# Transposing the last two tiles of batch 2 by DMA instead of TensorE, and holding the loads of batch 4 until they have landed

## The chip, the cores and the metric

The kernel runs on one core of one Trainium2 chip. The metric is device time in microseconds (us) of one execution. Before the change it is 290.95 us, the median of 3 runs (290.88 to 290.97). A profiled execution also has a *span*: from its first to its last instruction in the trace. The span is about 1.8 us shorter than the time.

## The reference

Per batch (8 of them) and head (8), linear attention without a softmax, an RMS norm, then one MLP block over the joined heads:

```python
kv = einsum('bhsd,bhse->bhde', k, v)            # 64 x 64 per head, s = 576
out = einsum('bhsd,bhde->bhse', q, kv)
x = out / sqrt(mean(out**2, -1) + 1e-6) * g_norm     # then heads joined: 576 x 512 per batch
xn = (x - mean(x)) / sqrt(var(x) + 1e-6) * g_ln
y = x + relu(xn @ w_ch1) @ w_ch2                 # 512 -> 2048 -> 512
```

## The kernel before

TensorE (PE) runs the two dense products batch after batch: `mm1` (`xT` by `w1`, L412) and `mm2` (`m` by `w2`, L428). The attention of later batches is cut into small pieces, which an agenda drops between groups of dense matmuls. A *slot* is one such group; a batch has 32. DVE (VectorE) and ACT (ScalarE) do the elementwise work, POOL (GpSimd) and SP (SyncE) issue most transfers, and PEld is PE's weight load. PE's products lie in PSUM until an *eviction* copies them out. A transfer tells of its landing by a *completion semaphore*, a counter that others wait for. Every tile of 128 rows of x must be turned (transposed) before `mm1` can use it, by PE through PSUM and an ACT copy, or by a DMA transpose on the SP queue:

```python
def turn(self, on_pe):
    dst = self.blk[2][:, :, self.ts * 128:(self.ts + 1) * 128]
    if on_pe:
        tp = ps_m.tile([128, nK, 128], bf16, tag="misc", name="tp")
        for kk in range(nK):
            nc.tensor.transpose(tp[:, kk, :], self.xc_t[:, kk * 128:(kk + 1) * 128], identity)
        nc.scalar.copy(dst, tp)
    else:
        nc.sync.dma_start_transpose(dst, self.xc_t)
...
def turn_q_dma(b):                       # q of a batch: a DVE copy, then one large DMA transpose
    q_p = ...
    nc.vector.tensor_copy(q_p.rearrange("p j h d -> p h j d"), q_in[b % NB])
    ...
    nc.sync.dma_start_transpose(q_t..., q_p...)
...
def load_batch(b, after=None):           # six loads on the POOL queue
    if after is not None:
        nc.gpsimd.tensor_copy(gate, after)   # one element: POOL waits for whoever writes `after`
    load(k_in[b % NB], k, b); load(v_in[b % NB], v, b); load(q_in[b % NB], q, b)
...
def plan_tile(s, make, turn_at, on_pe):  # attention of one tile from slot s on, turned at slot turn_at
    ...
at(36, lambda: kv_of(2))
at(36.5, lambda: turn_q_dma(2))
for j, s, tn in ((0, 44, 50), (1, 48, 54), (2, 53, 61), (3, 58, 67)):
    plan_tile(s, lambda j=j: main_tile(2, j), tn, j > 1)      # tiles 2 and 3 on PE
plan_tile(62, lambda: rem_tile(1), 69, False)
...
for b in range(3, B):
    s = 32 * b
    at(47 if b == 3 else s - 60,
       lambda b=b: load_batch(b, qts[b - 1][:1, J, HP - 1, 127:]))
    d = -41 if b == 3 else -45
    at(s + d, lambda b=b: kv_of(b))               # needs all of k and v of batch b
    at(s + d + 1.7, lambda b=b: turn_q_dma(b))
    for j in range(J):
        o = s + d + (10 if b == 3 else 13) + 5 * j
        plan_tile(o, lambda b=b, j=j: main_tile(b, j), o + 6, False)
```

Each 128-row output tile is evicted by DVE (L433) and stored by two transfers (L446, L447), nearly all on the SP queue; the last three pairs are shared by SP and ACT.

Of the kernel before, what the change touches and what calls it, by code (L numbers as in the profile page):

```python
# [14 lines left out]
def kernel(  # L15
# [11 lines left out]
    nc = tc.nc  # L27
# [10 lines left out]
    nK = Dm // 128  # L38
    nDe = Dh // 128
    HP = H // 2  # L40
# [3 lines left out]
    J, JJ, JP = 4, 5, 9  # L44
# [47 lines left out]
    def load(dst, t, b, h0=0, h1=H):  # L92
        nc.gpsimd.dma_start(dst[:64, h0:h1], lo(t, b, h0, h1))
        nc.gpsimd.dma_start(dst[64:, h0:h1, :J], up(t, b, h0, h1))

    def load_batch(b, after=None):
        if after is not None:
            nc.gpsimd.tensor_copy(gate, after)  # L98
        load(k_in[b % NB], k, b)
        load(v_in[b % NB], v, b)  # L100
        load(q_in[b % NB], q, b)
# [20 lines left out]
    gate = consts.tile([1, 1], bf16)  # L122
# [34 lines left out]
    load_w2(0)  # L157
    load_w2(1)
    load_batch(1)
    load_w2(2)  # L160
    load_w2(3)


    qts, held, blks, rstds, m1s, q_ps = {}, {}, {}, {}, {}, {}
# [35 lines left out]
    def turn_q_dma(b):  # L200
        q_p = kv_in.tile([128, JJ, H, D], bf16, tag="qp", bufs=2)
        nc.vector.tensor_copy(q_p.rearrange("p j h d -> p h j d"), q_in[b % NB])
        q_t = qt_pool.tile([128, JJ, HP, 128], bf16, tag="qt", name="qt")
        nc.sync.dma_start_transpose(
            q_t.rearrange("p j hp t -> p (j hp) t"), q_p.rearrange("p j h d -> p (j h d)"))
        qts[b] = q_t
# [31 lines left out]
    def kv_of(b):  # L238
        kv_ps = ps_m.tile([128, HP, D], f32, tag="misc", name="kv_ps")
        kvp = held[b] = kv_pack[b % 4]  # L240
        for hp in range(HP):
            for j in range(JJ):
                for hh in range(2):
                    h = 2 * hp + hh
                    nc.tensor.matmul(kv_ps[hh * D:hh * D + D, hp, :],  # L245
                                     lhsT=k_in[b % NB][:, h, j, :], rhs=v_in[b % NB][:, h, j, :],
                                     start=(j == 0), stop=(j == JJ - 1))
        nc.scalar.copy(kvp[:D, :, :D], kv_ps[:D])  # L248
        nc.scalar.copy(kvp[D:, :, D:], kv_ps[D:])

    def new_block(n, bufs):
        x_blk = xpool.tile([128, 4, Dm], f32, tag=f"x{n}", bufs=bufs, name="x_blk")
        st_blk = xpool.tile([128, 3, 4], f32, tag=f"st{n}", bufs=bufs, name="st_blk")
        xT_blk = xpool.tile([128, nK, 512], bf16, tag=f"xT{n}", bufs=bufs, name="xT_blk")
        return x_blk, st_blk, xT_blk
# [98 lines left out]
    def main_tile(b, j, pool=None, tag="ops"):  # L354
        q_t, kvp = qts[b], held[b]
        if b not in blks:
            blks[b] = new_block("main", 3)
        return Tile([(slice(0, 128), lambda hp: q_t[:, j, hp, :], kvp)], blks[b], j, pool, tag)

    def rem_tile(b):  # L360
        mms = []
        for half, bb in enumerate((b - 1, b)):
            qt, kp = qts.pop(bb), held.pop(bb)
            mms.append((slice(half * 64, (half + 1) * 64),
                        lambda hp, qt=qt: qt[:, J, hp, :64], kp))
        if "rem" not in blks:
            blks["rem"] = new_block("rem", 1)
        return Tile(mms, blks["rem"], b // 2)

    def plan_tile(s, make, turn_at, on_pe):  # L370
        box = []

        def first():
            t = make()
            box.append(t)
            t.o()
            t.sq()
            t.red()

        def second():  # L380
            t = box[0]
            t.y()
            t.x()
            t.xc()

        def third():
            box[0].var()

        def fourth():
            box[0].turn(on_pe)  # L390

        at(s, first)
        at(s + 2, second)
        at(s + 6, third)
        at(turn_at, fourth)
# [22 lines left out]
    def rstd_of(b):  # L418
        rstd = work.tile([128, 4], f32, tag="rstd", bufs=3, name="rstd")
        nc.scalar.activation(rstd, blks[b][1][:, 2, :], func=AF.Sqrt, scale=1.0 / Dm, bias=eps_sb)  # L420
        nc.vector.reciprocal(rstd, rstd)  # L421
        rstds[b] = rstd
# [45 lines left out]
    def at(slot, fn):  # L468
        agenda.setdefault(int(slot), []).append((slot, fn))
# [119 lines left out]
    def next_loads():  # L589
        nc.gpsimd.memset(k_in[0][64:, :, J], 0.0)  # L590
        nc.gpsimd.memset(v_in[0][64:, :, J], 0.0)
        load_batch(2)
# [30 lines left out]

    at(36, lambda: kv_of(2))
    at(36.5, lambda: turn_q_dma(2))
    for j, s, tn in ((0, 44, 50), (1, 48, 54), (2, 53, 61), (3, 58, 67)):
        plan_tile(s, lambda j=j: main_tile(2, j), tn, j > 1)
    plan_tile(62, lambda: rem_tile(1), 69, False)
    at(78, lambda: rstd_of(2))

    for b in range(3, B):
        s = 32 * b
        at(47 if b == 3 else s - 60,
           lambda b=b: load_batch(b, qts[b - 1][:1, J, HP - 1, 127:]))
        d = -41 if b == 3 else -45
        at(s + d, lambda b=b: kv_of(b))
        at(s + d + 1.7, lambda b=b: turn_q_dma(b))
# [3 lines that stand above are left out]
        if b % 2:  # L641
            plan_tile(s - 14, lambda b=b: rem_tile(b), s - 8, False)
        at(s + 14, lambda b=b: rstd_of(b))
# [59 lines left out]
```

## Time and profile before

| what | value |
|---|---|
| time, median | 290.95 us |
| span of the profiled run | 289.16 us |
| PE busy | 97% of the span |
| chain of waits that ended last | 91% PE |
| first product of the kernel (kv of batch 0) starts | 8.27 us |
| last eviction ends | 286.10 us |

The page of the kernel before: its first lines (busy us, share of the span, instructions) and the shares of the chain that ended last.

```profile
span 289.2 us, 5765 instructions
PE 279.8 (97%) x2289; PEld 158.9 (55%) x2315; DVE 149.8 (52%) x331; ACT 155.4 (54%) x338; POOL 40.9 (14%) x68
...
PE 91%; DMA 2%; DVE 2%; ACT 2%; issue 1%; DVEq 0%; POOLq 0%
```

PE is the limit. Only what leaves its stream, or makes it stand still, moves the time. The next fence is PE's timeline of the kernel before around the two tiles (start us, duration us, what).

```profile
78.95 0.39 PE L347 MATMUL tp<-identity,xc 128*128 128x128 bf16 x4
79.17 1.03 PE L428 MATMUL p<-w_sb,m 128*128 128x512 bf16 x4
...
82.22 1.04 PE L412 MATMUL p<-xT_blk,w_sb 128*128 128x256 bf16 x8
83.31 0.40 PE L270 MATMUL o_ps<-kv_pack,qt 128*128 128x128 bf16 x4
...
85.29 0.39 PE L347 MATMUL tp<-identity,xc 128*128 128x128 bf16 x4
85.51 0.71 PE L412 MATMUL p<-xT_blk,w_sb 128*128 128x256 bf16 x5
```

Four transposes last 0.39 us from the first start to the last end, but the next matmul starts 0.22 us after the first of them: that is what they cost. Note too the 1.09 us between the starts at 82.22 and 83.31. Eight matmuls of 256 columns at about 0.109 us need only 0.87. That gap of 0.22 us turned out to matter. The list of waits of the kernel before has it (us in total, times, longest) not at PE but at PEld, the weight load, which I had passed over:

```profile
PEld L270 <- DMA qt<-q_p: 0.3, 1, 0.3
```

POOL's timeline of the kernel before shows the hold of batch 4's loads: one copy that waits for the q transpose of batch 3, then the first load.

```profile
83.38 0.18 POOL L98 COPY gate<-qt 1x1 bf16<-1x1 bf16 x1 [16.93 <-DMA qt<-q_p]
84.57 0.68 POOL L93 DMA_DIRECT2D k_in<-in_k_dram  x1 [1.01 <-PE o_ps L270]
```

The landing times in the trace put the last v load of batch 4 at 97.60 us; PE starts `kv_of(4)` at 100.67.

### The profile page before, as it was taken

The numbers are of one execution on the slowest core, as the hardware profiler recorded it, in microseconds if no ns is written. First come the engines' busy times: TensorE is split into PE (matmuls) and PEld (weight loads), VectorE is DVE, ScalarE is ACT, GpSimd is POOL, SyncE is SP. The second block draws the span as 40 slices with busy tenths as digits, with TensorE's granted clock in tenths as the row PEclk, the third lists the DMA queues.
The fourth block names the chain that finished last, engine by engine and source line by source line (L and its number), as shares of the span: only waits on it lengthen the run. The fifth ranks groups of instructions, "written<-read, shape, count | busy, mean of one in ns | idle before, by whom it ended". The sixth has DMA issues, their size and how long they took to land.

```text
span 289.2 us, 5765 instructions
## 1 busy us (share of the span) xinstructions
PE 279.8 (97%) x2289; PEld 158.9 (55%) x2315; DVE 149.8 (52%) x331; ACT 155.4 (54%) x338; POOL 40.9 (14%) x68
## 2 busy tenths in 40 slices
PE   7889999999999999999999999999999999999995
PEld 3579755995569644445444444444444444444444
DVE  5774028838987783765366925762578300220022
ACT  3477854985469832882288418920894076016500
POOL 8522520031032003200410022000000000000000
PEclk9999999999999999999999999999999999999999
DMA  7999999569999929996997179937202510131033
GB/s 215 199 208 202 201 203 206 125 103 196 151 168 129 178 53 165 184 164 123 144 211 102 39 146 204 170 79 161 54 18 54 111 36 0 39 82 27 0 74 73
DMA packets 64890, 36.10 MB, mean 125 GB/s; under 512 B 32860, under 2 KB 59868, under 8 KB 64864
## 3 DMA queue, kind: packets, MB, share of 16 engines
q0 software_dynamic: 28528, 17.76, 46.0%
q1 hardware_dynamic: 35824, 17.25, 31.3%
q10 hardware_dynamic: 512, 0.72, 0.7%
q8 instruction: 18, 0.29, 0.4%
q14 instruction: 8, 0.07, 0.1%
HBM read 36.71 MB, written 9.44 MB: 160 GB/s over the span
## 4 chain that ended last, share of the span: by engine, by line
PE 91%; DMA 2%; DVE 2%; ACT 2%; issue 1%; DVEq 0%; POOLq 0%
PE p L428 43%; PE p L412 42%; PE o_ps L270 3%; DMA v_in<-in_v_dram 2%; PE kv_ps L245 2%; ACT m L415 1%; DVE x_blk L288 0%; DVE xc L546 0%; PE tp L347 0%; ACT sq L276 0%; ACT xT_blk L349 0%; PE tp L170 0%; ACT rms L307 0%; DVE ss L512 0%; PE tp L553 0%
## 5 line engine op out<-in xcount | busy, mean ns | idle before, releaser
L412 PE MATMUL p<-xT_blk,w_sb 128*128 128x128 bf16 (+2 forms) x1017 | 131.4, 285 | 0.8
L428 PE MATMUL p<-w_sb,m 128*128 128x512 bf16 (+2 forms) x590 | 126.8, 368 | 1.6 <-issue 1.0
L415 ACT ACTIVATE m<-p 128x512 bf16<-128x512 f32 x144 | 85.4, 596 | 43.9 <-PE p L412 41.8
L412 PEld LDWEIGHTS <-w_sb 128*128 128x128 bf16 x1024 | 78.6, 98 | 44.5 <-issue 1.1
L428 PEld LDWEIGHTS <-m 128*128 128x128 bf16 x608 | 56.8, 98 | 61.7
L433 DVE SCALAR_TENSOR_TENSOR o_sb<-p,rstd,x_blk 128x512 f32<-128x512 f32 (+2 forms) x38 | 27.3, 721 | 53.2 <-PE p L428 47.6
L276 ACT ACTIVATE sq<-o_ps 128x512 f32<-128x512 f32 x35 | 20.9, 596 | 42.1 <-PE o_ps L270 42.1
L297 DVE TENSOR_REDUCE ss<-sq 128x8 f32<-128x512 f32 x35 | 23.7, 678 | 11.4 <-ACT sq L276 11.4
L339 ACT ACTIVATE dev<-x_blk,st_blk 128x512 f32<-128x512 f32 x36 | 25.7, 714 | 4.6 <-DVE st_blk L325 4.4
L331 DVE SCALAR_TENSOR_TENSOR xc<-x_blk,st_blk,g_ln_sb 128x512 bf16<-128x512 f32 x34 | 25.6, 752 | 1.2
L302 DVE TENSOR_TENSOR y<-o_ps,inv 128x512 f32<-128x512 f32 x33 | 22.8, 692 | 3.0
L321 DVE SCALAR_TENSOR_TENSOR x_blk<-y,g_norm_sb 128x512 f32<-128x512 f32 x33 | 22.8, 692 | 1.1
L314 DVE RECIPROCAL inv<-rms 128x8 f32<-128x8 f32 x36 | 7.2, 201 | 24.8 <-ACT rms L307 24.8
L421 DVE RECIPROCAL rstd<-rstd 128x4 f32<-128x4 f32 x9 | 1.6, 174 | 34.7 <-ACT rstd L420 34.7
L98 POOL COPY gate<-qt 1x1 bf16<-1x1 bf16 x5 | 0.9, 176 | 113.2 <-DMA qt<-q_p 113.2
L307 ACT ACTIVATE rms<-ss,eps_sb 128x8 f32<-128x8 f32 x36 | 10.7, 297 | 8.0 <-DVE ss L297 7.7
L270 PEld LDWEIGHTS <-qt 128*128 128x128 bf16 (+1 forms) x156 | 10.2, 100 | 7.3 <-issue 1.7
L270 PE MATMUL o_ps<-kv_pack,qt 128*128 128x128 bf16 (+1 forms) x156 | 13.7, 220 | 0.1
L197 PE MATMUL p<-fill_sb 128*128 128x512 bf16 x26 | 7.8, 449 | 1.3 <-DVE eps_sb L137 1.2
L339 ACT ACTIVATION_READ_ACCUMULATOR dev<-x_blk,st_blk 128x1 f32 x36 | 6.9, 190 | 0.0
L248 ACT CAST kv_pack<-kv_ps 64x256 bf16<-64x256 f32 x7 | 2.6, 365 | 7.2 <-PE kv_ps L245 7.2
L245 PEld LDWEIGHTS <-k_in 128*64 128x64 bf16 x280 | 5.0, 112 | 2.6 <-issue 2.5
(79 smaller groups left out, 116.5 us busy)
## 6 DMA issues: line engine op xcount, KB each, us to landing
out_dram<-o_sb SPq DMA_DIRECT2D x70, 128.0 KB, 2.4
w_sb<-in_moe_w_ch_dram POOLq DMA_DIRECT2D x8, 512.0 KB, 14.0
k_in<-in_k_dram POOLq DMA_DIRECT2D x7, 320.0 KB, 5.8
v_in<-in_v_dram POOLq DMA_DIRECT2D x7, 320.0 KB, 10.2
q_in<-in_q_dram POOLq DMA_DIRECT2D x7, 320.0 KB, 13.0
q_in<-in_q_dram POOLq DMA_DIRECT2D x8, 256.0 KB, 13.3
k_in<-in_k_dram POOLq DMA_DIRECT2D x7, 256.0 KB, 7.4
v_in<-in_v_dram POOLq DMA_DIRECT2D x7, 256.0 KB, 11.0
```

The costliest lines, as they stand in the source:

```text
L245: nc.tensor.matmul(kv_ps[hh * D:hh * D + D, hp, :], lhsT=k_in[b % NB][:, h, j, :], rhs=v_in[b % NB][:, h, j, :], start=(j == 0), stop=(j = ...
L270: nc.tensor.matmul(flat[rows, hp * 128:(hp + 1) * 128], lhsT=lhsT_of(hp), rhs=kvp[:, hp, :], start=True, stop=True)
L276: nc.scalar.activation(self.sq_t, self.o_ps, func=AF.Square)
L297: nc.vector.tensor_reduce(self.ss, self.sq_t, axis=AX.X, op=ALU.add)
L302: nc.vector.tensor_mul(self.y_t, self.o_ps, self.inv().to_broadcast([128, H, D]))
L321: nc.vector.scalar_tensor_tensor(x_blk[:, ts].rearrange("p (h d) -> p h d", h=H), in0=self.y_t, scalar=1.0, in1=g_norm_sb.to_broadcast([12 ...
L331: nc.vector.scalar_tensor_tensor(self.xc_t, in0=x_blk[:, self.ts], scalar=st[:, 1, self.ts:self.ts + 1], in1=g_ln_sb, op0=ALU.add, op1=ALU ...
L339: nc.scalar.activation(dev, x_blk[:, ts], func=AF.Square, bias=st[:, 1, ts:ts + 1], accum_out=st[:, 2, ts:ts + 1])
L412: nc.tensor.matmul(p1[:, i, :], lhsT=w1_sb[:, kk, de * 128:(de + 1) * 128], rhs=blk[2][:, kk, sl], start=(kk == 0), stop=(kk == nK - 1))
L415: nc.scalar.activation(m1[:, de0:de0 + per, sl], p1, func=AF.Relu)
L428: nc.tensor.matmul(p2[:, c0:c1], lhsT=m1s[b][:, de, ts * 128:(ts + 1) * 128], rhs=w2_sb[:, de, c0:c1], start=(de == 0), stop=(de == nDe - 1))
L433: nc.vector.scalar_tensor_tensor(o_sb[:, c0:c1], in0=p2[:, c0:c1], scalar=rstds[b][:, ts:ts + 1], in1=blks[b][0][:, ts, c0:c1], op0=ALU.mu ...
```

## The change

The intent is to take the remaining PE transposes of batch 2 out of PE's stream. A DMA transpose is slow beside loads (in the kernel before one landed 9.7 us after its issue beside the loads of batch 4, the quickest 2.4 us), so the loads of batch 4 are held until tile 3's has landed. Tile 3 also moves to slightly earlier slots.

```diff
-    def load_batch(b, after=None):
-        if after is not None:
-            nc.gpsimd.tensor_copy(gate, after)
+    def load_batch(b, *after):
+        for element in after:
+            nc.gpsimd.tensor_copy(gate, element)
...
-    for j, s, tn in ((0, 44, 50), (1, 48, 54), (2, 53, 61), (3, 58, 67)):
-        plan_tile(s, lambda j=j: main_tile(2, j), tn, j > 1)
+    for j, s, tn in ((0, 44, 50), (1, 48, 54), (2, 53, 61), (3, 57.5, 64)):
+        plan_tile(s, lambda j=j: main_tile(2, j), tn, False)
...
-           lambda b=b: load_batch(b, qts[b - 1][:1, J, HP - 1, 127:]))
+           lambda b=b: load_batch(b, qts[b - 1][:1, J, HP - 1, 127:],
+                                  *([blks[2][2][:1, nK - 1, 511:]] if b == 4 else [])))
```

## The prediction

> **What bounds the kernel now.** TensorE. The page has PE busy 279.8 of 289.2 us (97%) at full granted clock; the chain of waits that ended last is 91% PE, mostly the two dense products (L428 43%, L412 42%). The list of waits has about 4 us of PE waits, most in the start-up. DVE (52%), ACT (54%) and the DMA engines are not the limit. Time falls only by what leaves PE's stream, and grows only by a transfer that makes PE stand still.
>
> **What the change removes.** Tiles 2 and 3 of batch 2 are no longer transposed on PE: 8 transposes and 8 weight loads, and two ACT evictions of 0.58 us. In the timeline the four transposes of a tile take 0.39 us from first start to last end, but they are pipelined: at 78.95 and at 85.29 us the surrounding product is displaced by 0.22 us each. All on PE's path: 0.44 us. PE did not wait for the evictions: worth nothing.
>
> **What it adds.** Two DMA transposes on the SP queue (issue 1.2 us, landing 2.4 us after issue at best, 3.8 median, 10.4 beside loads) and one tiny POOL copy. The order on SP is fixed: tile 2's goes between two pairs of output stores, tile 3's behind the second pair, before the one of the remainder tile. From before's issue times (q transpose until 81.4, stores 81.5 to 82.7) I work out: tile 2 issued at about 82.7, tile 3 at about 85.2, landed at 85.3 and 87.8. PE needs them at slot 72, about 90.1 us: slack of some 2 us, no wait, as no load is beside them. The Trainium skill, "DMA: Bandwidth & Descriptors", section "SWDGE vs HWDGE vs iDMA", says that these two feed different queues inside each DMA engine and take turns there; the trace agrees (a transpose beside loads landed after 9.7 us, one alone after 2.4).
>
> **What it moves.** The six loads of batch 4 begin at about 88.4 instead of 84.57 us. Before, the last v load landed 13.0 us after the first issue, at 97.60, and PE began kv of batch 4 at 100.67: slack 3.1 us, and the loads lose 3.8. But two transposes and a stretch of almost no traffic (91 to 93 us) lay in those 13 us; batches 3 and 6 took 9.3 and 10.0 us. After, the remainder tile's transpose is out of the way; I expect 10 to 12 us, so landing at 98.5 to 100.5, PE being there at 100.2. Most likely no wait, with one chance in three of a PE wait of about 1 us at kv of batch 4, never made up. q lands by 105 us, before its copy at about 106.
>
> **Sum.** 290.95 - 0.44 + about 0.1 of expected stall = 290.6 us. Range 290.1 to 291.6. Faster by 2% (5.8 us): 0.01; within 2%: 0.98; slower: 0.01.
>
> **What would show it.** PE instructions 16 fewer; no transposes at 79 and 85 us; POOL's hold ends near 88 us; first product of columns 256 to 511 of batch 2 without a wait; v of batch 4 landed before kv starts (right), or a PE wait for DMA v_in (wrong by its length).
>
> **What would make it wrong.** Tile 3's transpose landing later than 90 us (then PE waits at slot 72 and the loads slip further); loads of batch 4 taking 13 us again; the late q of batch 4 holding DVE, and through it the stores and the transpose of q; tile 3, a slot earlier, making DVE late with an eviction.

## The result, and the profile after

The changed kernel took 291.41 us, median of 4 runs (291.22 to 291.64), beside 290.94 us for the kernel before. The ratio is 1.0017, with a 95% interval from 0.9999 to 1.0034. (A ratio is the mean time of one kernel's fast runs over that of the other's of the same rounds, so it is not quite the ratio of the medians.) It is the same within 2%, and inside the predicted range, but the expected gain of 0.35 us is a loss of 0.47.

I cut each profiled execution into four pieces, and this cut decides nearly everything below:

- *head*: from the start of the span to the first kv product (code that the change does not touch);
- *body*: from there to the end of the last eviction;
- *end*: from there to the end of the span;
- *outside*: time less span.

The first two lines are of the kernel before, from the timelines of PE and DVE: the first kv product and the last eviction.

```profile
8.27 0.19 PE L224 MATMUL even<-v_in,k_in 64*64 64x64 bf16 x1 [1.50 <-DMA v_in<-in_v_dram]
...
285.75 0.35 DVE L433 SCALAR_TENSOR_TENSOR o_sb<-p,rstd,x_blk 128x128 f32<-128x128 f32 x1 [0.54 <-PE p L428]
```

The same two, and the span line of the page, of the changed kernel:

```profile
span 289.6 us, 5755 instructions
...
8.63 0.19 PE L224 MATMUL even<-v_in,k_in 64*64 64x64 bf16 x1 [0.52 <-DMA v_in<-in_v_dram]
...
285.86 0.35 DVE L433 SCALAR_TENSOR_TENSOR o_sb<-p,rstd,x_blk 128x128 f32<-128x128 f32 x1 [0.54 <-PE p L428]
```

| piece, us | before | changed | difference |
|---|---|---|---|
| head | 8.27 | 8.63 | +0.36 |
| body (285.75 + 0.35 - 8.27, and so on) | 277.83 | 277.58 | -0.25 |
| end (spans 289.16 and 289.64 unrounded) | 3.07 | 3.43 | +0.36 |
| outside (profiled run: 290.94 and 291.64 less span) | 1.78 | 2.00 | +0.22 |

The heads differ, so a time read in one profile compares with one in another only after the heads are taken off.

So the change gains in the body, as it was meant to, though less than the 0.44 us of PE work removed. It loses in two places that the prediction never looked at: the end, and outside the span. PE's timeline of the changed kernel shows where the gain shrank:

```profile
80.63 1.90 PE L428 MATMUL p<-w_sb,m 128*128 128x512 bf16 x8
82.36 1.04 PE L412 MATMUL p<-xT_blk,w_sb 128*128 128x256 bf16 x8
83.65 0.40 PE L270 MATMUL o_ps<-kv_pack,qt 128*128 128x128 bf16 x4 [0.24 <-DMA qt<-q_p]
83.88 2.35 PE L412 MATMUL p<-xT_blk,w_sb 128*128 128x256 bf16 x20
```

Both groups of transposes are gone. But from 82.36 to 83.65 it is 1.29 us, where before it was 1.09. Counted from the first kv product, PE starts these eight matmuls at 73.73 us, before at 73.95: arriving 0.22 us earlier, it waits 0.2 us longer for the q transpose of batch 3. That transpose is issued by a chain (an eviction, two stores, the q copy on DVE) that runs before the saved work and so does not become earlier: from the first kv product it is issued at 69.96 us, before at 69.95.

POOL's timeline of the changed kernel shows the new hold. The loads begin at 90.06 us:

```profile
88.88 0.18 POOL L98 COPY gate<-xT_blk 1x1 bf16<-1x1 bf16 x1 [4.98 <-DMA xT_blk<-xc]
90.06 0.68 POOL L93 DMA_DIRECT2D k_in<-in_k_dram  x1 [1.01 <-PE p L412]
```

The last v load landed at 99.71 us, PE started `kv_of(4)` at 100.78, and no wait appears there. The two DMA transposes landed 2.5 us after their issue. (PE's counts on the page fall from 2315 weight loads to 2307, as predicted, and from 2289 matmuls to 2282; a trace can miss a few matmuls.)

For the end, the list of waits of the SP queue, first of the kernel before:

```profile
SPq L698 <- DMA out_dram<-o_sb: 1.2, 2, 0.8
```

and of the changed kernel (us in total, times, longest):

```profile
SPq L699 <- DMA out_dram<-o_sb: 1.5, 1, 1.5
```

After its last store SP waits for the completion semaphores of all queues. In the trace's records these are nine instructions, each reading two semaphores in a fixed order, about 0.06 us apart. The transfers of SP and ACT take turns on eight of these semaphores. In the kernel before the last two stores complete on the two read last: SP has passed all the others while it waited, stops twice (for the landing of the second-last and of the last pair), and is done 0.14 us after the last landing. In the changed kernel two more SP transfers have turned the rotation by two. The last two stores now complete on semaphores read second and third, SP stops at the second for 1.5 us, and still has to read the other seven after the last landing; it is done 0.51 us after it.

### The profile page after: what moved, and what is told of

Read it like the earlier page. It is cut to its first block, busy times and chain, and to the rows that moved or that the text cites. A ratio compares the mean times of both kernels' runs of the same rounds, so it can differ in the third digit from the quotient of the medians.

```text
span 289.6 us, 5755 instructions
## 1 busy us (share of the span) xinstructions
PE 280.8 (97%) x2282; PEld 158.7 (55%) x2307; DVE 149.8 (52%) x331; ACT 154.4 (53%) x336; POOL 41.4 (14%) x69
## 4 chain that ended last, share of the span: by engine, by line
PE 69%; DMA 17%; issue 9%; POOL 2%; DVE 1%; POOLq 0%; DVEq 0%
PE p L428 33%; PE p L412 33%; DMA q_in<-in_q_dram 8%; DMA w_sb<-in_moe_w_ch_dram 5%; DMA v_in<-in_v_dram 3%; PE o_ps L270 2%; DMA qt<-q_p 2%; PE kv_ps L245 1%; POOL q_in L94 0%; DVE o_sb L433 0%; DVE q_p L202 0%; POOL v_in L93 0%; POOL v_in L94 0%; POOL k_in L93 0%; POOL q_in L93 0%
## 5 line engine op out<-in xcount | busy, mean ns | idle before, releaser
L197 PE MATMUL p<-fill_sb 128*128 128x512 bf16 x26 | 9.1, 512 | 1.3 <-DVE eps_sb L137 1.2
```

## The experiments

All ran correct. The table has every run: head, body and end in its profiled execution, *outside* as the mean of its runs (for the kernel before its profiled run; its later runs give means of 1.77 to 1.80), medians of the time, and the median of the kernel before in the same rounds.

| run | head | body | end | outside | time | before, same rounds |
|---|---|---|---|---|---|---|
| before | 8.27 | 277.83 | 3.07 | 1.78 | 290.94 | |
| changed | 8.63 | 277.58 | 3.43 | 2.02 | 291.41 | 290.94 |
| e1_before_plus2 | 9.05 | 277.79 | 3.43 | 1.75 | 291.35 | 291.23 |
| e2_after_plus6 | 8.32 | 277.58 | 3.04 | 1.96 | 290.97 | 291.23 |
| e3_after_nohold | 8.20 | 285.36 | 3.42 | 1.99 | 298.99 | 291.23 |
| e4_after_oldslots | 8.20 | 277.63 | 3.41 | 1.76 | 291.06 | 291.23 |
| e5_after_early_q | 8.26 | 277.19 | 3.40 | 2.02 | 290.82 | 291.12 |
| e6_after_best | 8.20 | 279.12 | 3.07 | 1.98 | 292.48 | 291.12 |
| e7_tile2_alone | 8.20 | 277.82 | 3.15 | 1.81 | 291.03 | 291.12 |
| e8_combined | 8.27 | 277.16 | 3.04 | 2.00 | 290.46 | 290.84 |
| e9_before_early_q | 8.95 | 277.60 | 3.06 | 1.78 | 291.38 | 290.84 |
| e10_combined_oldslots | 8.35 | 277.15 | 3.06 | 1.76 | 290.33 | 290.84 |
| e11_after_again | 8.18 | 277.57 | 3.44 | 1.98 | 291.19 | 290.90 |
| e12_before_2memsets | 8.18 | 277.61 | 3.05 | 2.02 | 290.85 | 291.01 |

Each kernel has one profiled execution, the changed kernel two. Where kernels differ only in what should not touch the body, it agrees to about 0.04 us (277.83 and 277.79 for before and e1; 277.58, 277.58 and 277.57 for changed, e2 and e11), and the end to about 0.04. The head does not: 8.18 to 9.05, and single times of the kernel before run from 290.77 to 291.91. So the pieces, not the medians, tell these experiments apart.

### Two and six more small transfers: the end (e1, e2)

Undo the suspected cause without the change, and cause it without the change.

```diff
+    spare = consts.tile([8, D], f32)
...
+    for i in range(2):          # e1, in the kernel before; range(6) in e2, in the changed kernel
+        nc.sync.dma_start(spare[i:i + 1, :], g_norm.rearrange("(a d) -> a d", a=1))
```

> The kernel before with two tiny extra transfers on the SP queue at the start, and nothing else. Theory A (end): the changed kernel loses at its end because two more transfers of the SP and ACT queues turn the rotation of completion semaphores by two, so that the last stores complete on the semaphores that SP reads second of nine, and SP still has to read the other seven, one after the other, after the last landing. Then this kernel loses the same at its end: time from the last eviction's end to the end of the span 3.4 us instead of 3.06, total about 291.3. Theory B (middle): the changed kernel's loss comes from its middle or is chance; then this kernel stays at 290.95, with 3.06 us at the end.

> The changed kernel with six tiny extra transfers on the SP queue at the start, so that with its own two the rotation is turned by eight, which is none. Theory A: the end takes 3.06 us again instead of 3.43, total 0.36 us under the changed kernel, about 291.05, or 290.7 if the 0.37 us that its profiled run lost at the start (v landing later) was chance. Theory B: no difference to the changed kernel, 291.4.

In e1 the end is 3.43 us and the body unchanged (277.79): two transfers that do nothing, 280 us earlier, cost the same 0.36 us. In e2 the rotation is turned by eight in all, which is none, and the end is 3.04 us. Theory A holds, theory B falls. The list of SP waits of e1:

```profile
SPq L701 <- DMA out_dram<-o_sb: 1.5, 1, 1.5
```

and of e2:

```profile
SPq L702 <- DMA out_dram<-o_sb: 1.2, 2, 0.8
```

The median of e1 (ratio 1.0003, interval 0.999 to 1.0017) would not have shown this; on that chip the head was scattering.

### Without the hold (e3)

```diff
-                                  *([blks[2][2][:1, nK - 1, 511:]] if b == 4 else [])))
+                                  *[]))
```

> The changed kernel without the hold: loads of batch 4 start when the q transpose of batch 3 has landed, as before. If the hold is what makes the DMA transposes cheap: loads start near 84.6 us, tile 3's transpose is issued near 86 and lands beside them after some 9.7 us, near 96; PE needs it near 90.3 and stands still for about 5 us: total 295 to 297. Rival (the hold is idle, a transpose ahead of most load traffic lands in time): no PE wait, total within 0.3 of 291.4.

It took 298.99 us (ratio 1.0265, interval 1.0246 to 1.0284). The loads began at 84.50 us, tile 3's transpose was issued at 85.78 and landed 9.6 us later. PE's timeline of e3, then two stretches of its windows (the column before the last two is the granted clock):

```profile
88.06 1.91 PE L412 MATMUL p<-xT_blk,w_sb 128*128 128x256 bf16 x16
95.44 4.91 PE L412 MATMUL p<-xT_blk,w_sb 128*128 128x256 bf16 x24 [5.47 <-DMA xT_blk<-xc]
```

```profile
90.00:96.00 6.00, 0.56 (x3) 0.44 (x4) 2.57 (x7) 1.22 (x4) 0.00 (x0) 0.75 1.52 144
96.00:102.00 6.00, 6.00 (x42) 4.69 (x40) 0.50 (x1) 2.80 (x6) 0.00 (x0) 0.68 1.17 163
```

The wait is 5.5 us, as the first theory had it, but the body grew by 7.78. The missing 2.3 us come after the wait: 24 matmuls took 4.91 us, where 24 at 0.109 would take 2.6. The Trainium skill, "TensorE: Matmul & The Clock Gate", section "Part 1: The HAM clock gate", says that an idle window of about 3.4 us puts the array back to half its clock. This run agrees in the main: the granted clock is 0.75 and 0.68 in these stretches, 1.00 before them and after. Narrower windows show how these means come about:

```profile
93.00:95.00 2.00, 0.00 (x0) 0.00 (x0) 0.91 (x2) 0.00 (x0) 0.00 (x0) 0.50 1.00 139
...
97.00:99.80 2.80, 2.80 (x15) 2.00 (x14) 0.00 (x0) 1.19 (x2) 0.00 (x0) 0.50 1.33 187
99.80:102.00 2.20, 2.20 (x24) 1.99 (x23) 0.50 (x1) 1.60 (x4) 0.00 (x0) 1.00 0.88 122
```

The clock fell to half about 3.0 us after PE's last matmul (which ended at 89.97), a little sooner than the page's figure, and was full again only at 99.8, over 4 us after PE resumed. So this wait cost more than itself; how short a wait would still do so was not measured. The hold is what makes the change possible at all.

### Tile 3 at its old slots (e4)

```diff
-(3, 57.5, 64)
+(3, 58, 67)
```

> The changed kernel with tile 3 of batch 2 at its old slots (58 and 67 instead of 57.5 and 64). The moved slot put tile 3's DVE work ahead of an eviction, which came 3.4 us later, and with it the stores and both transposes by about 0.9 us. Theory A: none of this is on PE's path, so time stays at 291.4 within 0.15, while the hold ends about 0.9 us earlier. Rival: the late eviction or the late loads cost time somewhere, and this kernel is 0.2 us or more faster in the middle.

The body is 277.63, against 277.58: the late eviction and late loads cost nothing there. The timelines of SP and POOL of e4 show the transposes and the loads about 1 us earlier than in the changed kernel (issues at 83.61, 86.22 and 90.06 there). But 0.43 us of that is the head (8.63 there, 8.20 here). The moved slots are worth the other 0.5 us, not the 0.9 of the expectation; e11, the changed kernel again with a head of 8.18, bears this out below.

```profile
82.67 1.30 SPq L351 DMA_TRANSPOSE xT_blk<-xc  x1
...
85.29 5.16 SPq L351 DMA_TRANSPOSE xT_blk<-xc  x3
```

```profile
87.89 0.27 POOL L98 COPY gate<-xT_blk 1x1 bf16<-1x1 bf16 x1 [4.37 <-DMA xT_blk<-xc]
89.08 0.68 POOL L93 DMA_DIRECT2D k_in<-in_k_dram  x1 [0.93 <-PE o_ps L270]
```

The surprise is in the last piece: *outside* is 1.76 us here, 2.02 in the changed kernel. I come back to it with e12.

### q of batch 3 earlier (e5, e9), and tile 2 alone (e7)

e5 puts the q copy of batch 3 ahead of an eviction on DVE in the changed kernel; e9 does the same in the kernel before.

```diff
-        at(s + d + 1.7, lambda b=b: turn_q_dma(b))
+        at(s + d + (0.9 if b == 3 else 1.7), lambda b=b: turn_q_dma(b))
```

e7 is the kernel before with tile 2 alone turned by DMA, and the hold on its landing.

```diff
-        plan_tile(s, lambda j=j: main_tile(2, j), tn, j > 1)
+        plan_tile(s, lambda j=j: main_tile(2, j), tn, j > 2)
...
-           lambda b=b: load_batch(b, qts[b - 1][:1, J, HP - 1, 127:]))
+           lambda b=b: load_batch(b, qts[b - 1][:1, J, HP - 1, 127:],
+                                  *([blks[2][2][:1, nK - 1, 383:384]] if b == 4 else [])))
```

> The changed kernel with the q copy of batch 3 put one slot earlier on DVE, ahead of an eviction, so that its DMA transpose is issued and lands about 1 us earlier. Theory (absorbed gain): in the changed kernel half of the 0.44 us that PE saves is taken back by a new wait of the first tile of batch 3 for that q transpose, which PE now reaches earlier; then the body here (first kv product to the end of the last eviction) is 277.36 us instead of the changed kernel's 277.58, without a PE wait for q. Rival (a transposed tile is worth only 0.11 us of PE, nothing is absorbed): the body stays at 277.58. The end stays at 3.43 us in both.

> The kernel before with tile 2 of batch 2 alone turned by DMA, the loads of batch 4 held for it, tile 3 on PE and at its old slots. Theory (absorbed gain): its 0.22 us are lost in the wait for q, body 277.8 as before (277.83), with a PE wait of about 0.2 us for q. Rival: body 277.7 or less (each tile gives 0.11 to 0.13). One more SP transfer: the rotation turns by one; theory for the end: again about 3.4 us, as one of the last two stores then completes on the semaphore read second.

> The kernel before with the earlier q copy of batch 3 alone. The changed kernel gained 0.39 us from it, more than the 0.22 expected, so the kernel before may hold some of that wait already. Theory: body 277.83 - 0.2 = 277.6 us, so that on top of the earlier q copy the DMA turning is worth its full 0.44 us. Rival: the earlier q copy is worth the whole 0.39 here too (277.44), and the turning only 0.25. The end stays at 3.07.

PE's timeline of e5, where nothing is left between the groups (81.99 to 82.86 is 0.87 us):

```profile
81.99 1.04 PE L412 MATMUL p<-xT_blk,w_sb 128*128 128x256 bf16 x8
82.86 0.39 PE L270 MATMUL o_ps<-kv_pack,qt 128*128 128x128 bf16 x4
```

The bodies make a table of two by two:

| body, us | q as it was | q earlier | difference |
|---|---|---|---|
| tiles 2 and 3 on PE | 277.83 | 277.60 | -0.23 |
| tiles 2 and 3 by DMA | 277.58 | 277.19 | -0.39 |
| difference | -0.25 | -0.41 | |

Where q is early, the turning is worth 0.41 us, close to the 0.44 that the timeline promised. Where q is late, 0.16 of it is taken by the longer wait for q (0.2 in the timelines). The expectation of e5 (277.36) missed that the kernel before already held 0.22 us of the same wait; e9 shows this directly. e7 fits: tile 2's saving lies before the wait for q, and alone it is worth nothing (277.82, with a PE wait for q of 0.27 us). Tile 3's lies behind it. e7's end is a small miss: 3.15 us, not 3.4. Turned by one, only the SP half of the last pair completes on an early semaphore. It lands 0.26 us before the ACT half, so SP has read most of the others by then.

### Versions meant to beat both (e6, e8, e10)

e6 avoids the wait for q by moving the tiles of batch 3 one slot later; e8 uses the earlier q copy instead; e10 is e8 with tile 3 at its old slots. All three restore the rotation by giving one pair of output stores to the POOL queue, which is idle by then:

```diff
-        nc.sync.dma_start(dsts[0][:, c0:c1], o_sb[:64, c0:c1])
-        (nc.scalar if both else nc.sync).dma_start(dsts[1][:, c0:c1], o_sb[64:, c0:c1])
+        first = nc.gpsimd if (b, ts) == (7, 0) else nc.sync
+        first.dma_start(dsts[0][:, c0:c1], o_sb[:64, c0:c1])
+        (nc.scalar if both else first).dma_start(dsts[1][:, c0:c1], o_sb[64:, c0:c1])
...
-            o = s + d + (10 if b == 3 else 13) + 5 * j        # e6 alone
+            o = s + d + (11 if b == 3 else 13) + 5 * j
```

> A version meant to beat both: the changed kernel with the tiles of batch 3 one slot later (no wait for q) and one pair of output stores of the last batch issued from the POOL queue, so that the number of SP and ACT transfers, and with it the rotation of the completion semaphores, is that of the kernel before. Theory: body 277.36 us, end 3.06 us, together 0.47 us under the kernel before: about 290.5 where that takes 290.95. Rival for the body as in the run before it: 277.58. Rival for the end (the two extra transposes themselves, not the rotation): 3.43.

> The changed kernel with the earlier q copy of batch 3 (body 277.19 us measured) and one pair of stores of batch 7 from the POOL queue (end 3.07 us measured in another kernel). Theory: both hold together, as they act on different stretches: body 277.19, end 3.07, about 0.65 us under the kernel before. Rival: the slack of the late v loads is used up (0.13 us left in the run with the earlier q copy) and some executions lose it: body above 277.3, or times spread by more than 0.5 us.

> As the combined kernel, but tile 3 of batch 2 at its old slots, which ends the hold about 0.9 us earlier and so gives the v loads of batch 4 about 1 us of slack before PE needs them. Theory: body 277.2 to 277.25, end 3.07, time within 0.1 us of the combined kernel. Rival: the moved slots matter once q comes early, and the body is longer by 0.2 us or more.

e6 failed in the body: 279.12 us (time ratio 1.0045, interval 1.0031 to 1.0059, and all five runs within 0.4 us). Its list of PE waits has two new ones:

```profile
PE kv_ps L245 <- DMA v_in<-in_v_dram: 1.1, 1, 1.1
...
PE p L412 <- DMA xT_blk<-xc: 0.6, 1, 0.6
```

Tile 3's transpose took 4.3 us to land in this run instead of 2.5. PE waited 0.6 us for it, the hold ended 90.4 us into the span, and the v loads of batch 4 came 1.1 us late. These two waits account for 1.7 of the 1.76 us that the body is over the expected 277.36. So the danger that the prediction gave one chance in three is real. The changed kernel escapes it by the 1.07 us between 99.71 and 100.78 in its first profile, by 0.68 in e11 and 0.35 in e2: a thin margin. Why the transpose was slow is open. In the packet records a 16 KB instruction fetch begins at 87.72 us, inside this transpose; in the changed kernel, e4, e5, e8, e10 and e11, where tile 3 lands in 2.5 us, the fetch begins only after the landing (in e4 and e10 by 0.2 us or less). That fits the fetch as the cause, but no run tests it. Its end, 3.07 us, is as expected.

e8 and e10 did as expected in body and end. e10 is the better by its pieces: body 277.15, end 3.06, outside 1.76, median 290.33 us beside 290.84 (ratio 0.9987, interval 0.9973 to 1.0000). The interval reaches 1, so that the times alone do not prove the gain over the kernel before; the body and the end do. Its lead over e8 (median 290.46, ratio 0.9990, interval 0.9977 to 1.0002) lies outside the span alone. Its v loads land at 99.43, PE needs them at 100.08.

### The changed kernel again (e11)

> The changed kernel itself, once more. Theory: of the 0.47 us that its first runs lost, 0.36 are chance (the first kv product began at 8.63 instead of 8.27 us, in code that the change does not touch); body 277.58 and end 3.43 us come again, and over five runs it lies about 0.1 us over the fast runs of the kernel before, with single runs of both scattered over some 0.7 us. Rival: the late start belongs to the changed kernel (its program lies elsewhere in memory): the first product again at 8.6 us or later, all runs at 291.2 or more, 0.4 us over before.

Body and end came again (277.57, 3.44), and the head was 8.18: the late start of the first profile was chance. The transposes and the first load, from its timelines of SP and POOL, are 0.5 us later than in e4, whose head is the same within 0.02 us:

```profile
83.14 1.30 SPq L351 DMA_TRANSPOSE xT_blk<-xc  x1
...
85.77 5.47 SPq L351 DMA_TRANSPOSE xT_blk<-xc  x3
...
89.58 0.68 POOL L93 DMA_DIRECT2D k_in<-in_k_dram  x1 [1.01 <-PE p L412]
```

Its last v load landed at 99.64 us, and PE started `kv_of(4)` at 100.32. The loss was 0.29 us in the medians, not 0.1 (ratio 1.0011, interval 0.9997 to 1.0024): the expectation had left out the piece outside the span. With it the sum is -0.26 + 0.37 + 0.21 = +0.32.

### What is outside the span (e12)

All seven profiled executions with tile 3 at the moved slots have 0.2 us more outside the span than the six without. In the trace their DVE programs count 438 instructions, the others 436 or 437: another order needs other waits (104 semaphore waits in the changed kernel, 103 in e4, 102 before). e12 makes the kernel before as long as that.

```diff
+    spare = consts.tile([128, 2], f32)
...
+    for i in range(2):
+        nc.vector.memset(spare[:, i:i + 1], 0.0)
```

> All kernels with the moved slots show 0.2 us more outside the profiled span (time less span 1.96 to 2.02 us, the others 1.75 to 1.81). They are also the ones whose DVE program has 438 instructions in the trace, the others have 437 or fewer (the kernel before 436). This is the kernel before with two tiny DVE memsets in idle DVE time at the start, so 438. Theory (length of the DVE program): time less span about 2.0 us, span as before. Rival (something else about the moved slots): about 1.78.

The four runs lay 1.97 to 2.06 us over their spans (given to 0.1 us), the kernel before of the same rounds 1.78 to 1.83. In the profiled executions, whose spans are exact, the eight kernels with 438 lie at 1.91 to 2.00, the six others at 1.77 or 1.78. So the 0.2 us do not need the moved slots; they came with two more DVE instructions. Two things stay open. No record shows what the core does in that time, or why one instruction from 437 to 438 should matter; that the count is the cause is a correlation, and no run adds a single memset or the tile alone. And e12 changed something else: the 8 bytes per partition of the new tile. These two are the q transposes of the kernel before, then of e12 (duration of the issue in ns, minimum, median, maximum; then landing in us):

```profile
L204 SPq DMA_TRANSPOSE qt<-q_p x6: 3076/3172/3227, 56.9 to 193.1; - x6
...
DMA to landing us min/median/max: 5.0/5.1/6.8
```

```profile
L207 SPq DMA_TRANSPOSE qt<-q_p x6: 2542/2570/2657, 56.8 to 192.8; - x6
...
DMA to landing us min/median/max: 4.1/4.3/5.9
```

All six q transposes are 0.6 us shorter, and through the one of batch 3 the body lost its wait for q (277.61, the 277.60 of e9). That the cause is where the buffers lie in memory is an argument from the edit; no run separates it from the memsets. The other kernels with 438 instructions have no such tile, or one of 256 bytes, and long q transposes, so the placement is an unlikely cause of the 0.2 us outside.

## Why the prediction was right or wrong

- **PE is the limit: right.** Every body difference is a change in PE's stream or a wait of PE.
- **"All on PE's path: 0.44 us": the gross size was right, the net was not.** With q out of the way it is 0.41 us (e5 against e9). In the changed kernel it is 0.25, because PE ran into the q transpose of batch 3 sooner. The prediction asked whether x and v would arrive in time and did not ask it of q, although the list of waits before already had one of 0.3 us for it.
- **Landing of the two transposes: outcome right, times too early by 0.8 to 1.0 us in the first profile, by 0.4 to 0.6 in e11's.** Predicted issues at 82.7 and 85.2, landings at 85.3 and 87.8; measured 83.61, 86.22, 86.08 and 88.76, but with the head 0.36 us later than before, and in e11 83.14, 85.77, 85.66 and 88.28. What the head does not explain is the moved slot, which put tile 3's DVE work ahead of an eviction and so delayed its stores on SP. With the old slots (e4) the issues are at 82.67 and 85.29, the landings at 85.16 and 87.77.
- **"No wait, as no load is beside them": right, and the hold is worth more than the prediction said.** Without it the landing takes 9.6 us, and the medians of e3 and the changed kernel are 7.6 us apart.
- **v of batch 4: right.** No wait; 9.65 us from the first issue to v's landing, expected were 10 to 12, while the loads began 1.7 us later than predicted (1.2 in e11): the transpose landed 1 us later (0.5 in e11), and 1.3 us passed from its landing to the first load, where the prediction had 0.6. The margin before PE was 1.07 us in the first profile and 0.68 in e11; e6 shows the wait that was feared.
- **The sum: this step failed.** "290.95 - 0.44 + about 0.1" took PE's body for the whole time. The mis-sized or missing terms are: PE -0.25 instead of -0.44; stall 0 instead of +0.1; the end +0.36 instead of 0 (two more SP transfers turn the semaphore rotation; e1, e2); outside the span +0.2 instead of 0 (it came with a DVE program of 438 instructions; e4, e12; why is open). That is about +0.3 us, as e11 measured. The rest of the first +0.47 fits the head, which scatters: the spans of these four runs go from 289.2 to 289.6 us. That the time lay in the predicted range all the same is luck: the range was 1.5 us wide, for an expected gain of 0.35 that came out as a loss.

## What to carry to other kernels

When a saving is a few tenths of a microsecond, cut the profile into head, body, end and what is outside the span before explaining anything: each moved here by as much as the saving, for reasons of its own. When work leaves the limiting engine, look for the next arrival that it will now run into, and move that too. Adding or removing a transfer on a queue can change the order in which the final waits fall; count them, and keep the last stores on the semaphores that are read last.

## What the Trainium skill lacked or had wrong

- The final wait for completion semaphores is serial, in a fixed order, about 0.06 us a step, so the end depends on how far the number of transfers has turned the eight semaphores: 3.07 us (before), 3.15 with one more (e7), 3.43 with two (e1), and 3.04 again with eight (e2). "DMA: Bandwidth & Descriptors" belongs to it; I found it on no page.
- The time outside the profiled span is not the same for all forms of one kernel: means of 1.75 to 1.81 us with up to 437 DVE instructions in the trace, 1.96 to 2.02 with 438; the cause is open. "Runtime: NRT & Kernel Launch" would be the place; I found it on no page.
- "VectorE: DVE Perf Modes", section "The three transpose paths", gives a 128x128 transpose 390 ns on TensorE and 1309 ns by DMA. What a PE transpose costs between other matmuls is far less: four of them displaced the stream by 0.22 us. A DMA transpose of a 128x512 tile took 1.3 us to issue and 2.5 us to land with no load beside it (4.3 once, in e6), but 9.6 us beside six loads (e3).
- The q transposes (128x2560, SBUF to SBUF by DMA) became a fifth shorter (issue of 3.17 to 2.57 us) with an edit that added 8 bytes per partition and two memsets (e12), while the smaller xT ones stayed at 1.20 us. "DMA: Bandwidth & Descriptors", section "DMA Transpose (X-bar)", has 32-byte alignment as its constraint on where the data lie in SBUF; whether the placement is the cause here stays open.
